# A Fourier and gated convolution kernel: where 64-bit weights are narrowed, and in how many operations

## The chip, the cores and the metric

The kernel runs on one core of a Trainium2 chip. The metric is device time in microseconds (us), as the median of several executions on the chip; a single profiled execution has a span, which is some 1.8 us shorter than its time. In the text TensorE, VectorE, ScalarE and GpSimd are the four compute engines; in the profile they are PE (and PEld for its weight loads), DVE, ACT and POOL. SP is the engine that issues most of the transfers.

## The reference, cut to what matters

```python
def _attn_ref(x):                        # x: 8 batches, 3136 positions, 256 features, float32
    X = np.fft.fft(x, axis=1)
    X = np.fft.fft(X, axis=2)
    return X.real.astype(np.float32)

def _moe_ref(x, w_in, conv_w, w_out):    # 256 -> 1024 -> 256, kernel of 3 along the positions
    h = np.maximum(x @ w_in, 0.0)
    conv_out = ...                       # three taps of h along the positions, per feature
    gate = 1.0 / (1.0 + np.exp(-conv_out))
    return (h * gate @ w_out).astype(np.float32)
```

The three weights arrive as 64-bit floats. The kernel works in 32-bit floats and has to narrow them itself: 256 x 1024 first weights, 3 x 1024 taps, 1024 x 256 second weights.

## The kernel before

The kernel first **folds** x of a batch by its symmetries (VectorE), multiplies the folded x with tables of cosines and sines (the DFT along the positions, TensorE, in nine units), and leaves a pair of matrices, pt and qt. The feature DFT is folded into the first weights: `G` is the product of a small DFT matrix `dm` with `win`. Then 256 **steps** follow: 8 batches x 4 chunks of positions x 8 groups of 128 hidden features. A step multiplies pt and qt with G (`pa`, `pb`), combines them into h, computes the taps, the sigmoid and the gate, and multiplies with the second weights `wout`. Folds and DFT of the next batch are spread over the steps of the batch before it, as work on the side.

The start, and the narrowing before the change:

```python
    def narrow(dst, raw, ng):            # ten operations, scratch tiles f, g, h
        ts, tt, st = ng.tensor_scalar, ng.tensor_tensor, ng.scalar_tensor_tensor
        ...
        ts(out=fi, in0=hi, scalar1=20, scalar2=0x7FF, op0=lsr, op1=ALU.bitwise_and)
        ts(out=fi, in0=fi, scalar1=896, scalar2=1151, op0=ALU.max, op1=ALU.min)
        ts(out=fi, in0=fi, scalar1=23, scalar2=-0x40000000, op0=lsl, op1=ALU.bitwise_xor)
        ts(out=gi, in0=hi, scalar1=-0x80000000, scalar2=None, op0=ALU.bitwise_and)
        st(out=fi, in0=fi, scalar=0x7FFFFFFF, in1=gi, op0=ALU.bitwise_and, op1=ALU.bitwise_or)
        ts(out=gi, in0=lo, scalar1=1, scalar2=None, op0=lsr)
        st(out=g, in0=gi, scalar=2.0 ** -51, in1=f, op0=ALU.mult, op1=ALU.mult)
        ts(out=hi_, in0=hi, scalar1=3, scalar2=0x7FFFF8, op0=lsl, op1=ALU.bitwise_and)
        tt(out=fi, in0=fi, in1=hi_, op=ALU.bitwise_or)
        tt(out=dst, in0=f, in1=g, op=ALU.add)

    ...
    for t in range(2):                   # first weights, whole rows: 1 MB each, first in ScalarE's queue
        todo += load_weight(win[t], words(moe_w_in)[t * P:(t + 1) * P].unsqueeze(1), nc.vector, nc.scalar)
    for h in range(2):
        for f in load_ops(0, h, nc.sync, nc.scalar):     # x of batch 0
            f()
    todo += load_weight(cw24, ...)       # taps
    nc.scalar.dma_start(out=dm, in_=dft_dim[:, :, 0:2])
    for par in (1, 0):
        load_tables(par)                 # odd tables, then even ones
    for f in todo:                       # narrow all first weights, then the taps
        f()
    late_w = load_weight(wout, words(moe_w_out)..., nc.vector, nc.sync)   # three blocks, for later
    for par in (1, 0):
        mend_tables(par, half)           # ScalarE copies of the odd tables
    ...                                  # G, ge, cw: all of them here
    for f in fold_ops(0):
        f()
    for h in range(2):
        for f in load_ops(1, h, nc.sync, nc.sync):
            f()
    begin, us, row = units(0)
    begin()
    for i, u in enumerate(us):           # DFT of batch 0
        u.matmuls(0, 1)
        u.copy()
        if i == 4:
            row()
        u.fin()
        if i == 4:
            spread(0)
        for g in late_w[i::len(us)]:     # a block of second weights after units 0, 1 and 2
            g()
```

`row` and `spread` carry one row of qt through DRAM and spread it over the partitions (`er`, `ed`, `eb`); each step's `pa` is seeded with it.

Of the kernel before, what the change touches and what calls it, by code (L numbers as in the profile page):

```python
# [10 lines left out]
I32 = mybir.dt.int32  # L11
AF = mybir.ActivationFunctionType
# [22 lines left out]
def kernel(  # L35
# [70 lines left out]
    def load_ops(b, h, eng, eng2):  # L106

        def plain():
            t = xp.tile([P, 8, 2, D], F32, name="xh", tag="xh")
            xh[b, h] = t  # L110
            eng.dma_start(out=t[0:NP, 0:4], in_=bass.AP(
                tensor=x.tensor, offset=x.offset + (b * S + 1 + 2 * h) * D,
                ap=[[HQ * D, NP], [Q4 * D, 4], [1, 2 * D]]))
            if h == 1:
                for s in range(8):
                    r = s if s < 4 else (8 - s) % 4
                    eng2.dma_start(out=t[NP:KR, s],
                                   in_=x[b:b + 1, r * Q4:r * Q4 + 1].to_broadcast([1, 2, D]))
# [248 lines left out]
    def narrow(dst, raw, ng):  # L367

        k, n = dst.shape

        ts, tt, st = ng.tensor_scalar, ng.tensor_tensor, ng.scalar_tensor_tensor
        lsl, lsr = ALU.logical_shift_left, ALU.logical_shift_right
        f, g, h = [hp.tile([P, HW], F32, name="nt", tag="h")[0:k, 0:n] for _ in range(3)]
        fi, gi, hi_ = [t.bitcast(I32) for t in (f, g, h)]
        lo, hi = raw[:, :, 0], raw[:, :, 1]

        ts(out=fi, in0=hi, scalar1=20, scalar2=0x7FF, op0=lsr, op1=ALU.bitwise_and)
        ts(out=fi, in0=fi, scalar1=896, scalar2=1151, op0=ALU.max, op1=ALU.min)
        ts(out=fi, in0=fi, scalar1=23, scalar2=-0x40000000, op0=lsl, op1=ALU.bitwise_xor)
        ts(out=gi, in0=hi, scalar1=-0x80000000, scalar2=None, op0=ALU.bitwise_and)  # L380
        st(out=fi, in0=fi, scalar=0x7FFFFFFF, in1=gi, op0=ALU.bitwise_and, op1=ALU.bitwise_or)

        ts(out=gi, in0=lo, scalar1=1, scalar2=None, op0=lsr)
        st(out=g, in0=gi, scalar=2.0 ** -51, in1=f, op0=ALU.mult, op1=ALU.mult)
        ts(out=hi_, in0=hi, scalar1=3, scalar2=0x7FFFF8, op0=lsl, op1=ALU.bitwise_and)
        tt(out=fi, in0=fi, in1=hi_, op=ALU.bitwise_or)
        tt(out=dst, in0=f, in1=g, op=ALU.add)

    def load_weight(dst, src, ng, eng):

        k, nc_, n = dst.shape
        if src.dtype == F32:
            eng.dma_start(out=dst, in_=src)
            return []
        raw = wp.tile([P, nc_ * n, 2], I32, name="raw", tag="w")[0:k]
        eng.dma_start(out=raw.rearrange("p (c n) e -> p c (n e)", c=nc_), in_=src)
        to = dst.rearrange("p c n -> p (c n)")
        w = nc_ * n
        parts = -(-w // HW)
        cuts = [slice(w * i // parts, w * (i + 1) // parts) for i in range(parts)]  # L400
        return [(lambda c=c: narrow(to[:, c], raw[:, c], ng)) for c in cuts]

    def words(w):
        return w if w.dtype == F32 else w.bitcast(I32)

    ident = gp.tile([3 * NF, 3 * NF], F32, name="ident", tag="g")
    make_identity(nc, ident)
    dm = gp.tile([P, 2, 2, P], F32, name="dm", tag="g")
    cw24 = gp.tile([3 * NF, 1, P], F32, name="cw24", tag="g")
# [4 lines left out]
    wout = const.tile([P, NF, D], F32, name="wout")  # L414
    win = pqp.tile([P, 2, F // 2 + 256], F32, name="win", tag="pt"), pqp.tile([P, 2, F // 2 + 256], F32, name="win", tag="qt")
    win = [t.rearrange("p a f -> p (a f)")[:, 0:F].unsqueeze(1) for t in win]
    todo = []
    for t in range(2):
        todo += load_weight(win[t], words(moe_w_in)[t * P:(t + 1) * P].unsqueeze(1), nc.vector, nc.scalar)
    for h in range(2):  # L420
        for f in load_ops(0, h, nc.sync, nc.scalar):
            f()
    todo += load_weight(cw24, words(moe_conv_w).rearrange("k (m p) -> (k m) p", m=NF).unsqueeze(1),
                        nc.vector, nc.scalar)
# [3 lines left out]
    for f in todo:  # L428
        f()
    late_w = load_weight(wout, words(moe_w_out).rearrange("(c p) o -> p c o", p=P), nc.vector, nc.sync)  # L430

    for par in (1, 0):
        mend_tables(par, half)
    G = const.tile([P, 2, F], F32, name="G")
    for g in range(2):
        for c in range(0, F, 512):
            p = psa.tile([P, 512], F32, name="pa", tag="pa") if g else spare()
            for t in range(2):
                mm(p, dm[:, t, g, :], win[t][:, 0, c:c + 512], t == 0, t == 1)
            nc.scalar.copy(out=G[:, g, c:c + 512], in_=p)  # L440

    ge = const.tile([P, NF], F32, name="ge")
    p = spare()
    for m in range(NF):
        for t in range(2):
            mm(p[:, m:m + 1], win[t][:, 0, m * P:(m + 1) * P], dm[:, t, 1, P - 1:P], t == 0, t == 1)
    nc.scalar.copy(out=ge, in_=p[:, 0:NF])
    cw = const.tile([P, 3, NF], F32, name="cw")
    p = spare()
# [80 lines left out]
    for f in fold_ops(0):  # L530
        f()
# [147 lines left out]
```

## Time and profile before

| | before |
|---|---|
| time, median of the first 3 runs | 1336.36 us (1335.93 to 1339.71) |
| span of the profiled run | 1334.3 us |
| PE, DVE, ACT, POOL busy | 91%, 88%, 66%, 35% |
| first h | 90.4 us (its second half stands in the chain of waits at 90.88) |
| length of batches 0 to 6, first h to first h | 165.9, 160.0, 157.9, 154.8, 154.8, 154.3, 147.9 us |
| batch 7 | 132.5 us from its first h to its last (31 steps), 148.3 to the end of the span |

The page names no engine that is full, because it averages a start, in which nearly everything waits, with a body, in which TensorE and VectorE are both almost full. So one reads the start and the body apart. The table of windows does this. Its columns are the window, its length, busy us (and instructions) of PE, PEld, DVE, ACT and POOL, the granted clock, the share of the transfer engines that is busy, and GB/s.

```profile
80.00:90.00 10.00, 1.40 (x2) 0.83 (x3) 0.79 (x2) 1.38 (x3) 3.22 (x7) 0.69 0.27 81
90.00:100.00 10.00, 6.22 (x10) 2.65 (x9) 9.52 (x12) 6.53 (x10) 1.86 (x2) 0.50 0.00 0
100.00:110.00 10.00, 8.29 (x21) 5.17 (x21) 9.93 (x14) 5.81 (x10) 3.46 (x7) 0.61 0.00 2
```

### The profile page before, as it was taken

The page shows a single profiled execution, that of the slowest core. Times are in us where ns is not written, and L with a number is a line of the kernel's source. Part 1 is how long each engine was busy: PE and PEld are TensorE (multiplying, and loading weights), DVE is VectorE, ACT ScalarE, POOL GpSimd, SP SyncE. Part 2 cuts the span into 40 slices and gives each one's busy share as a digit, 9 for nine tenths or more (in the row PEclk, how much of TensorE's full clock was granted, in tenths as well). Part 3 has the DMA queues.
Part 4 walks back from the last instruction along what each step waited for, and adds up shares of the span by engine and source line. Part 5 has one row for each costly group of instructions (what it writes and reads, how often), then busy time and mean ns, then how long its engine had stood idle before and what let it go on. Part 6 is the DMA issues. An engine that isn't in the chain of part 4 may idle for free.

```text
span 1334.3 us, 15340 instructions
## 1 busy us (share of the span) xinstructions
PE 1214.4 (91%) x4914; PEld 892.2 (67%) x4914; DVE 1175.9 (88%) x1664; ACT 887.0 (66%) x1558; POOL 462.1 (35%) x507
## 2 busy tenths in 40 slices
PE   0748899989899999999999999999999999999998
PEld 0425677767676777777676777767677777776766
DVE  6969999998998999998999899999899888878885
ACT  0225666667666677776767777776777767777775
POOL 2415525242532435242523335242332223222222
PEclk9968999999999999999999999999999999999999
DMA  7601202021120102120102102120001000100001
GB/s 227 176 25 37 85 25 65 32 64 35 54 67 24 52 26 71 49 75 25 60 13 74 50 25 73 48 75 0 25 24 48 27 24 25 34 30 22 24 20 43
DMA packets 46840, 66.02 MB, mean 49 GB/s; under 512 B 5600, under 2 KB 35196, under 8 KB 46504
## 3 DMA queue, kind: packets, MB, share of 16 engines
q1 hardware_dynamic: 41012, 49.80, 11.8%
q0 software_dynamic: 5120, 12.85, 3.2%
q10 hardware_dynamic: 628, 2.40, 0.6%
q8 instruction: 38, 0.62, 0.2%
q14 instruction: 42, 0.34, 0.1%
HBM read 39.24 MB, written 25.74 MB: 49 GB/s over the span
## 4 chain that ended last, share of the span: by engine, by line
DVE 50%; PE 22%; ACT 12%; issue 12%; DMA 3%; POOL 1%; DVEq 0%; ACTq 0%; POOLq 0%; SPq 0%
DVE g L498 16%; DVE h L486 15%; PE po L89 11%; ACT g L492 6%; PE pd L89 4%; DVE g L509 4%; PE pa L89 4%; PE pb L89 4%; DVE xh L158 3%; ACT os L525 2%; DVE xh L147 2%; DVE w L174 2%; DMA out_dram<-os 1%; ACT nb L485 1%; ACT pa L466 1%
## 5 line engine op out<-in xcount | busy, mean ns | idle before, releaser
L89 PE MATMUL po<-wout,g 128*128 128x256 f32 (+2 forms) x3200 | 735.9, 380 | 0.7 <-POOL g L508 0.7
L89 PEld LDWEIGHTS po<-wout,g 128*128 128x128 f32 (+2 forms) x3200 | 602.9, 188 | 149.1 <-issue 19.0
L498 DVE SCALAR_TENSOR_TENSOR g<-h,cw,g 128x770 f32<-128x770 f32 (+2 forms) x512 | 537.1, 1049 | 82.0 <-ACT g L492 72.3
L508 POOL TENSOR_TENSOR g<-g,h 128x385 f32<-128x385 f32 (+1 forms) x256 | 295.0, 1152 | 776.9 <-ACT g L501 634.1
L485 ACT ACTIVATE nb<-pb 128x386 f32<-128x386 f32 (+4 forms) x512 | 227.6, 499 | 147.2 <-PE pb L89 145.8
L501 ACT ACTIVATE g<-g 128x770 f32<-128x770 f32 (+2 forms) x256 | 221.1, 864 | 149.1 <-DVE g L498 148.6
L486 DVE CUSTOM_DVE_ANT_0 h<-pa,nb 128x386 f32<-128x386 f32 (+4 forms) x512 | 265.7, 561 | 50.4 <-PE pa L89 31.9
L492 ACT ACTIVATE g<-h,cw 128x770 f32<-128x770 f32 (+2 forms) x256 | 243.6, 952 | 46.9 <-DVE h L486 30.3
L89 PE MATMUL pa<-pt,G 128*128 128x386 f32 (+2 forms) x512 | 223.7, 518 | 43.8 <-ACT pa L466 43.6
L89 PE MATMUL pb<-qt,G 127*128 127x386 f32 (+2 forms) x512 | 215.8, 502 | 1.6 <-ACT nb L485 1.5
L89 PEld LDWEIGHTS pa<-pt,G 128*128 128x128 f32 x512 | 91.0, 191 | 144.7 <-ACT pa L466 101.4
L509 DVE TENSOR_TENSOR g<-g,h 128x385 f32<-128x385 f32 (+2 forms) x256 | 155.0, 606 | 0.5 <-ACT g L501 0.5
L466 ACT ACTIVATE pa<-eb,ge 128x386 f32<-128x386 f32 (+2 forms) x256 | 146.9, 574 | 8.1 <-DMA eb<-ed 8.1
L89 PE MATMUL pd<-tab,w 99*128 99x196 f32 (+2 forms) x448 | 123.1, 381 | 17.7 <-ACT g L492 6.1
L89 PEld LDWEIGHTS pb<-qt,G 127*128 127x128 f32 x512 | 94.7, 192 | 27.6 <-issue 4.5
L89 PEld LDWEIGHTS pd<-tab,w 99*128 99x128 f32 (+1 forms) x448 | 80.0, 189 | 44.7 <-ACT g L492 24.2
L122 POOL DMA_INDIRECT xh<-in_x_dram,idx x64 | 85.3, 1333 | 16.4 <-issue 12.2
L525 ACT COPY os<-po 128x256 f32<-128x256 f32 (+2 forms) x200 | 58.4, 384 | 13.5 <-DMA out_dram<-os 8.8
L158 DVE TENSOR_TENSOR xh<-xh 98x1024 f32<-98x1024 f32 (+1 forms) x32 | 51.1, 1603 | 0.1
L147 DVE TENSOR_TENSOR xh<-xh 98x1020 f32<-98x1020 f32 (+1 forms) x32 | 46.6, 1466 | 0.0
L89 PE MATMUL po<-win,dm 128*128 128x512 f32 x8 | 5.7, 872 | 38.9 <-DMA dm<-dft_dim_dram 38.9
L174 DVE TENSOR_TENSOR w<-xh 98x508 f32<-98x508 f32 (+1 forms) x32 | 37.5, 1172 | 0.1
(84 smaller groups left out, 352.8 us busy)
## 6 DMA issues: line engine op xcount, KB each, us to landing
out_dram<-os SPq DMA_DIRECT2D x184, 128.0 KB
xh<-in_x_dram SPq DMA_DIRECT2D x16, 784.0 KB
eb<-ed SPq DMA_DIRECT2D x16, 193.0 KB
tab<-dft_seq_dram SPq DMA_DIRECT2D x4, 601.8 KB
raw<-in_moe_w_in_dram ACTq DMA_DIRECT2D x2, 1024.0 KB
raw<-in_moe_w_out_dram SPq DMA_DIRECT2D x1, 2048.0 KB
eb<-ed SPq DMA_DIRECT2D x8, 209.0 KB
eb<-ed SPq DMA_DIRECT2D x8, 192.5 KB
```

The source lines that it names most:

```text
L89: nc.tensor.matmul(o, l, r, start=start, stop=stop, skip_group_check=True)
L122: nc.gpsimd.indirect_dma_start(out=xh[b, h][0:NP, 4 + m].rearrange("p q d -> p (q d)"), out_offset=None, in_=bass.AP(tensor=x.tensor, offs ...
L158: vt(flat(to, to + 2), flat(0, 2), flat(2, 4), op=op)
L466: act(pa[s][:, 0:n], eb[b, c], AF.Copy, scale=ge[:, f:f + 1])
L485: act(nb[:, i, cols], p[:, cols], AF.Copy, scale=-1.0 if i else 1.0)
L486: nc.vector._custom_dve(TENSOR_ADD_SAT, out=to, in0=a[:, cols], in1=nb[:, i, cols], s0=BIG, s1=0.0)
L492: act(gs[s], hs[s][:, 0:n], AF.Copy, scale=cw[:, 0, s[2]:s[2] + 1])
L498: stt(out=g, in0=h[:, k:k + n], scalar=cw[:, k, f:f + 1], in1=g, op0=ALU.mult, op1=ALU.add)
L501: act(gs[s], gs[s], AF.Sigmoid)
L508: gt(g[:, m:n], g[:, m:n], h[:, m + 1:n + 1], op=ALU.mult)
L509: vt(g[:, 0:m], g[:, 0:m], h[:, 1:m + 1], op=ALU.mult)
L525: nc.scalar.copy(out=osb[0:m, j % 2], in_=pt[0:m, j % 2])
```

## The change

Its intent: to start the folds as early as x is there. Only half of the first weights' columns is loaded and narrowed before the folds; the other half follows inside the DFT of batch 0, and the second weights only inside steps 1 to 8, a block of 256 columns in each. The ten operations become eight, which work in place in the raw words and in the destination. The loads stand in another order. Batch 1 is loaded and folded four steps later, and the windows of folds and DFT of the later batches move up to five steps.

```diff
-    def load_ops(b, h, eng, eng2):
+    def load_ops(b, h, eng):           # single rows ahead of the large load, all on SP's queue
...
+    def narrow(dst, raw):
+        ts = nc.vector.tensor_scalar
+        lo, hi = raw[:, :, 0], raw[:, :, 1]
+        lof, hif, d = lo.bitcast(F32), hi.bitcast(F32), dst.bitcast(I32)
+        ts(out=d, in0=hi, scalar1=20, scalar2=0x7FF, op0=lsr, op1=ALU.bitwise_and)
+        ts(out=d, in0=d, scalar1=-896, scalar2=0, op0=ALU.add, op1=ALU.max)
+        ts(out=d, in0=d, scalar1=23, scalar2=None, op0=lsl)
+        stt(out=d, in0=hi, scalar=-0x80000000, in1=d, op0=ALU.bitwise_and, op1=ALU.bitwise_or)
+        stt(out=lof, in0=lo.bitcast(U32), scalar=2.0 ** -52, in1=dst, op0=ALU.mult, op1=ALU.mult)
+        ts(out=hi, in0=hi, scalar1=3, scalar2=0x7FFFF8, op0=lsl, op1=ALU.bitwise_and)
+        vt(hi, hi, d, op=ALU.bitwise_or)
+        vt(dst, hif, lof, op=ALU.add)
...
+    w_in = Weight(win, moe_w_in.rearrange("(t p) n -> p t n", p=P), wp, "w")
+    w_in.load((0, 2), (0, H), nc.scalar)           # H = F // 2: half of the columns, one load
     for h in range(2):
-        for f in load_ops(0, h, nc.sync, nc.scalar):
+        for f in load_ops(0, h, nc.sync):
             f()
     nc.scalar.dma_start(out=dm, in_=dft_dim[:, :, 0:2])
     for par in (1, 0):
         load_tables(par)
+    w_cv.load((0, 1), (0, P), nc.scalar)
+    w_in.load((0, 2), (H, F), nc.scalar)           # the other half, one load
...
+    for t in range(2):
+        w_in.narrow(t, (0, H))
     for f in fold_ops(0):
         f()
-    for h in range(2):
-        for f in load_ops(1, h, nc.sync, nc.sync):
-            f()
+    w_cv.narrow(0, (0, P))
+    blocks(0)                                      # first half of G
+    for par in (1, 0):
+        mend_tables(par, half)
...                                                # in the DFT of batch 0:
         if i == 4:
             spread(0)
-        for g in late_w[i::len(us)]:
-            g()
+            taps()
+            w_in.narrow(0, (H, F))
+        if i == 6:
+            w_in.narrow(1, (H, F))
+    blocks(1)                                      # second half of G
+    w_out = Weight([wout[:, c] for c in range(NF)], moe_w_out..., wp, "w")
+    for c in range(0, NF, 2):
+        w_out.load((c, c + 2), (0, D), nc.sync)
...
+    for c in range(NF):
+        at(1 + c, "dve", lambda c=c: w_out.narrow(c, (0, D)))
+    for h in range(2):
+        for j, fn in enumerate(load_ops(1, h, nc.sync)):
+            at(3 * h + (j + 1) // 2, "load", fn)
...
-    end = 0
+    end = 4
     for b in range(1, B):
-        stop = per * (b - 1) + max(12 - 4 * (b - 1), 2)
+        stop = per * (b - 1) + max(21 - 4 * b, 2)
         fold_at[b] = (end, stop - end)
         dft_at[b] = (stop, per * b - 3 - stop)
```

More of the change, by code (lines that the diff above doesn't have):

```diff
@@ L11 @@
 I32 = mybir.dt.int32
+U32 = mybir.dt.uint32
 AF = mybir.ActivationFunctionType
@@ L110, in plain @@
             xh[b, h] = t
+            if h == 1:
+                for s in range(8):
+                    r = s if s < 4 else (8 - s) % 4
+                    eng.dma_start(out=t[NP:KR, s],
+                                  in_=x[b:b + 1, r * Q4:r * Q4 + 1].to_broadcast([1, 2, D]))
             eng.dma_start(out=t[0:NP, 0:4], in_=bass.AP(
@@ L113, in plain @@
                 ap=[[HQ * D, NP], [Q4 * D, 4], [1, 2 * D]]))
-            if h == 1:
-                for s in range(8):
-                    r = s if s < 4 else (8 - s) % 4
-                    eng2.dma_start(out=t[NP:KR, s],
-                                   in_=x[b:b + 1, r * Q4:r * Q4 + 1].to_broadcast([1, 2, D]))
         def mirrored(m):
@@ L363 @@
     HN = max(c.k1 - c.k0 for c in chunks)
-    def narrow(dst, raw, ng):
-        k, n = dst.shape
-        ts, tt, st = ng.tensor_scalar, ng.tensor_tensor, ng.scalar_tensor_tensor
+    def narrow(dst, raw):
+        ts = nc.vector.tensor_scalar
         lsl, lsr = ALU.logical_shift_left, ALU.logical_shift_right
-        f, g, h = [hp.tile([P, HW], F32, name="nt", tag="h")[0:k, 0:n] for _ in range(3)]
-        fi, gi, hi_ = [t.bitcast(I32) for t in (f, g, h)]
         lo, hi = raw[:, :, 0], raw[:, :, 1]
-        ts(out=fi, in0=hi, scalar1=20, scalar2=0x7FF, op0=lsr, op1=ALU.bitwise_and)
-        ts(out=fi, in0=fi, scalar1=896, scalar2=1151, op0=ALU.max, op1=ALU.min)
-        ts(out=fi, in0=fi, scalar1=23, scalar2=-0x40000000, op0=lsl, op1=ALU.bitwise_xor)
-        ts(out=gi, in0=hi, scalar1=-0x80000000, scalar2=None, op0=ALU.bitwise_and)
-        st(out=fi, in0=fi, scalar=0x7FFFFFFF, in1=gi, op0=ALU.bitwise_and, op1=ALU.bitwise_or)
-        ts(out=gi, in0=lo, scalar1=1, scalar2=None, op0=lsr)
-        st(out=g, in0=gi, scalar=2.0 ** -51, in1=f, op0=ALU.mult, op1=ALU.mult)
-        ts(out=hi_, in0=hi, scalar1=3, scalar2=0x7FFFF8, op0=lsl, op1=ALU.bitwise_and)
-        tt(out=fi, in0=fi, in1=hi_, op=ALU.bitwise_or)
-        tt(out=dst, in0=f, in1=g, op=ALU.add)
@@ L389, in load_weight @@
-    def load_weight(dst, src, ng, eng):
-        k, nc_, n = dst.shape
-        if src.dtype == F32:
-            eng.dma_start(out=dst, in_=src)
-            return []
-        raw = wp.tile([P, nc_ * n, 2], I32, name="raw", tag="w")[0:k]
-        eng.dma_start(out=raw.rearrange("p (c n) e -> p c (n e)", c=nc_), in_=src)
-        to = dst.rearrange("p c n -> p (c n)")
-        w = nc_ * n
-        parts = -(-w // HW)
-        cuts = [slice(w * i // parts, w * (i + 1) // parts) for i in range(parts)]
-        return [(lambda c=c: narrow(to[:, c], raw[:, c], ng)) for c in cuts]
@@ L403, in words @@
-    def words(w):
-        return w if w.dtype == F32 else w.bitcast(I32)
+        lof, hif, d = lo.bitcast(F32), hi.bitcast(F32), dst.bitcast(I32)
[4 more added lines that the diff above has]
+        stt(out=lof, in0=lo.bitcast(U32), scalar=2.0 ** -52, in1=dst, op0=ALU.mult, op1=ALU.mult)
@@ new lines, in narrow, with __init__, load @@
+        ts(out=hi, in0=hi, scalar1=3, scalar2=0x7FFFF8, op0=lsl, op1=ALU.bitwise_and)
+        vt(hi, hi, d, op=ALU.bitwise_or)
+        vt(dst, hif, lof, op=ALU.add)
+    class Weight:
+        def __init__(self, dst, src, pool, tag):
+            self.dst, self.src = dst, src
+            k, c, n = dst[0].shape[0], len(dst), dst[0].shape[1]
+            self.raw = None
+            if src.dtype != F32:
+                self.raw = pool.tile([P, c, n, 2], I32, name="raw", tag=tag)[0:k]
+                self.src = src.bitcast(I32)
+        def load(self, cs, cols, eng):
+            c0, c1 = cs
+            i0, i1 = cols
+            if self.raw is None:
+                for c in range(c0, c1):
+                    eng.dma_start(out=self.dst[c][:, i0:i1], in_=self.src[:, c, i0:i1])
+            else:
+                eng.dma_start(out=self.raw[:, c0:c1, i0:i1].rearrange("p c n e -> p c (n e)"),
+                              in_=self.src[:, c0:c1, 2 * i0:2 * i1])
+        def narrow(self, c, cols):
+            i0, i1 = cols
+            if self.raw is not None:
+                narrow(self.dst[c][:, i0:i1], self.raw[:, c, i0:i1])
@@ L406 @@
+    H = F // 2
     ident = gp.tile([3 * NF, 3 * NF], F32, name="ident", tag="g")
@@ L408 @@
     dm = gp.tile([P, 2, 2, P], F32, name="dm", tag="g")
-    cw24 = gp.tile([3 * NF, 1, P], F32, name="cw24", tag="g")
+    cw24 = gp.tile([3 * NF, P], F32, name="cw24", tag="g")
     half = const.tile([P, 1], F32, name="half")
@@ L413 @@
     nc.gpsimd.tensor_scalar(out=half, in0=half, scalar1=0.5, scalar2=0.5, op0=ALU.mult, op1=ALU.add)
-    wout = const.tile([P, NF, D], F32, name="wout")
-    win = pqp.tile([P, 2, F // 2 + 256], F32, name="win", tag="pt"), pqp.tile([P, 2, F // 2 + 256], F32, name="win", tag="qt")
-    win = [t.rearrange("p a f -> p (a f)")[:, 0:F].unsqueeze(1) for t in win]
-    todo = []
-    for t in range(2):
-        todo += load_weight(win[t], words(moe_w_in)[t * P:(t + 1) * P].unsqueeze(1), nc.vector, nc.scalar)
+    win = [pqp.tile([P, NK], F32, name="win", tag=tag)[:, 0:F] for tag in ("pt", "qt")]
+    w_in = Weight(win, moe_w_in.rearrange("(t p) n -> p t n", p=P), wp, "w")
+    w_in.load((0, 2), (0, H), nc.scalar)
     for h in range(2):
-        for f in load_ops(0, h, nc.sync, nc.scalar):
+        for f in load_ops(0, h, nc.sync):
             f()
-    todo += load_weight(cw24, words(moe_conv_w).rearrange("k (m p) -> (k m) p", m=NF).unsqueeze(1),
-                        nc.vector, nc.scalar)
     nc.scalar.dma_start(out=dm, in_=dft_dim[:, :, 0:2])
@@ L427, with blocks, taps @@
         load_tables(par)
-    for f in todo:
-        f()
-    late_w = load_weight(wout, words(moe_w_out).rearrange("(c p) o -> p c o", p=P), nc.vector, nc.sync)
-    for par in (1, 0):
-        mend_tables(par, half)
-    G = const.tile([P, 2, F], F32, name="G")
-    for g in range(2):
-        for c in range(0, F, 512):
+    w_cv = Weight([cw24], moe_conv_w.rearrange("k (m p) -> (k m) p", m=NF).unsqueeze(1), gp, "g")
+    w_cv.load((0, 1), (0, P), nc.scalar)
+    w_in.load((0, 2), (H, F), nc.scalar)
+    wout = const.tile([P, NF, D], F32, name="wout")
+    G = const.tile([P, 2, F], F32, name="G")
+    ge = const.tile([P, NF], F32, name="ge")
+    cw = const.tile([P, 3, NF], F32, name="cw")
+    def blocks(i):
+        c = slice(i * H, (i + 1) * H)
+        for g in range(2):
             p = psa.tile([P, 512], F32, name="pa", tag="pa") if g else spare()
             for t in range(2):
-                mm(p, dm[:, t, g, :], win[t][:, 0, c:c + 512], t == 0, t == 1)
-            nc.scalar.copy(out=G[:, g, c:c + 512], in_=p)
-    ge = const.tile([P, NF], F32, name="ge")
-    p = spare()
-    for m in range(NF):
-        for t in range(2):
-            mm(p[:, m:m + 1], win[t][:, 0, m * P:(m + 1) * P], dm[:, t, 1, P - 1:P], t == 0, t == 1)
-    nc.scalar.copy(out=ge, in_=p[:, 0:NF])
-    cw = const.tile([P, 3, NF], F32, name="cw")
-    p = spare()
-    mm(p[:, 0:3 * NF], cw24[:, 0], ident, True, True)
-    nc.scalar.copy(out=cw.rearrange("p k m -> p (k m)"), in_=p[:, 0:3 * NF])
+                mm(p, dm[:, t, g, :], win[t][:, c], t == 0, t == 1)
+            nc.scalar.copy(out=G[:, g, c], in_=p)
+        p = spare()
+        ms = slice(i * NF // 2, (i + 1) * NF // 2)
+        for m in range(ms.start, ms.stop):
+            for t in range(2):
+                mm(p[:, m:m + 1], win[t][:, m * P:(m + 1) * P], dm[:, t, 1, P - 1:P], t == 0, t == 1)
+        nc.scalar.copy(out=ge[:, ms], in_=p[:, ms])
+    def taps():
+        p = spare()
+        mm(p[:, 0:3 * NF], cw24, ident, True, True)
+        nc.scalar.copy(out=cw.rearrange("p k m -> p (k m)"), in_=p[:, 0:3 * NF])
     rows = out.rearrange("b s d -> (b s) d")
@@ L527, in mm2 @@
         gs.pop(s)
+    for t in range(2):
+        w_in.narrow(t, (0, H))
     for f in fold_ops(0):
         f()
-    for h in range(2):
-        for f in load_ops(1, h, nc.sync, nc.sync):
-            f()
+    w_cv.narrow(0, (0, P))
+    blocks(0)
+    for par in (1, 0):
+        mend_tables(par, half)
     begin, us, row = units(0)
@@ L544 @@
             spread(0)
-        for g in late_w[i::len(us)]:
-            g()
+            taps()
[3 more added lines that the diff above has]
+    blocks(1)
+    w_out = Weight([wout[:, c] for c in range(NF)], moe_w_out.rearrange("(c p) o -> p c o", p=P), wp, "w")
+    for c in range(0, NF, 2):
+        w_out.load((c, c + 2), (0, D), nc.sync)
     steps = [(b, c, f) for b in range(B) for c in range(len(chunks)) for f in range(NF)]
@@ L569 @@
                 c1 = cs[7 * h + 6] + 1
-                for j, fn in enumerate(load_ops(b + 1, h, nc.sync, nc.sync)):
+                for j, fn in enumerate(load_ops(b + 1, h, nc.sync)):
                     at(c1 + (j + 1) // 2, "load", fn)
```

## The prediction

> **What bounds the kernel now.** I read the page's strip of 40 slices first. In it a digit is the busy share of 33 us.
>
> ```profile
> PE   0748899989899999999999999999999999999998
> DVE  6969999998998999998999899999899888878885
> ```
>
> From the fourth slice on both TensorE (PE) and VectorE (DVE) are nearly full, so the body is a balance; the loose time is in slices one to three. So next the timeline of the start (start us, duration us, engine, line, operation, tiles, idle before it).
>
> ```profile
> 7.95 0.61 DVE L377 TENSOR_SCALAR nt<-raw 128x512 int32<-128x512 int32 x1 [7.95 <-DMA raw<-in_moe_w_in_dram]
> 8.59 0.43 DVE L378 TENSOR_SCALAR nt<-nt 128x512 int32<-128x512 int32 x1
> ...
> 12.83 0.69 DVE L387 TENSOR_TENSOR win<-nt 128x512 f32<-128x512 f32 x1
> 13.44 0.42 DVE L377 TENSOR_SCALAR nt<-raw 128x512 int32<-128x512 int32 x1
> ...
> 34.53 2.33 DVE L147 TENSOR_TENSOR xh<-xh 98x1020 f32<-98x1020 f32 x2
> ...
> 40.28 3.36 ACT L211 ACTIVATE tab<-tab 99x784 f32<-99x784 f32 x4 [8.60 <-DMA tab<-dft_seq_dram]
> ...
> 51.98 8.70 PE L89 MATMUL po<-tab,w 99*128 99x196 f32 x32 [0.17 <-POOL w L178]
> ...
> 60.59 0.87 DVE L387 TENSOR_TENSOR wout<-nt 128x682 f32<-128x682 f32 x1
> 61.37 0.56 DVE L289 TENSOR_TENSOR qt<-as,po 128x392 f32<-128x392 f32 x1
> ```
>
> DVE narrows the 64-bit first weights from 8 to 29.4, waits for the taps, and only at 34.5 starts the folds of batch 0, which end at 51.8 (17.3 us). DFT matmuls start at 52 and are then paced by DVE, which slips three blocks of second weights, 7.25 us each, between their results. From the chain of waits, what follows (start, duration, who):
>
> ```profile
> 77.13 1.91 DMA er<-qt
> 79.17 0.53 POOL er L317
> ...
> 84.53 3.41 DMA eb<-ed
> 87.97 0.59 ACT pa L466
> 88.60 1.67 PE pa L89 x2
> 90.88 0.55 DVE h L486
> ```
>
> The first of 256 steps computes h at 90.88. The path to it is DVE, then a row that travels through DRAM. Now the body, again in the chain of waits:
>
> ```profile
> 105.53 1.02 DVE h L486 x2
> ...
> 110.79 1.01 DVE h L486 x2
> ...
> 1213.03 1.03 DVE h L486 x2
> ...
> 1217.11 1.03 DVE h L486 x2
> ```
>
> A step with one fold operation takes 5.26 us, a bare one 4.08. The table of windows has DVE busy 9.93 of 10 us in 100-110, 120-130 and 130-140 alike: in the first steps DVE is the bound, without slack. By first h of each batch, batches last 165.9, 160.0, 157.9, 154.8, 154.8, 154.3, 147.9 and some 132.5 us: with neither folds nor DFT 132.5; the DFT adds about 15.4, and folds add some 7 when they run beside a DFT but 14.4 (12 x 1.2) in batch 0, where they run alone.
>
> [...] reads of raw (every second word) take 0.42 us, no more than contiguous ones, and the stores into qt, also every second word, take 0.56 us for 392 elements, what 1.07 ns per element plus 0.15 gives. [...] The large table loads have 49 rows[...]: the windows show 176 GB/s and DMA share 0.44 (7/16) at 22-27, where they run alone. [...] here the granted clock was 0.82 to 0.84 in 50-80 and 0.50 in 90-100, so I take DFT durations from this start and not from the body.
>
> **The change part by part.**
> 1. *Eight operations for ten.* Four one-source and four two-source operations: at 512 columns 4 x 0.43 + 4 x 0.69 = 4.48 us in place of 5.30. At 256 columns, from 0.21/0.28 us at 128 columns and 0.43/0.69 at 512, I estimate 0.28 and 0.42, so 2.80 us a block. All narrowing: 4 x 4.48 + about 2.0 (taps) + 8 x 2.80 = 42.3 us, against 4 x 5.30 + 2.4 + 3 x 7.25 = 45.4. Only 3 us are truly removed; the rest moves.
> 2. *Start.* The first half of the first weights is again 1 MB at the head of its queue, but its runs are half as long, beside x in another queue: 9.5 us (an estimate, from 8 before). Two blocks end at 18.5; by then the first half of x, requested first, should be there. Folds run straight on, 17.3 us, to 36. The other candidate is the tables: each of seven engines carries 2.4 MB/7 = 343 KB of them, plus its share of x, weights and dm, some 350 KB; at 176/7 = 25 GB/s this is 28 us after the first issue, plus waits of later loads for earlier ones: landed at 34. The four table copies (3.7) bring this to 38. Tables are the later: DFT starts at 38, not 52.
> 3. *DFT.* Units 0 to 3 take 8.7 us as before, now with no second weights between: qt complete at 48 (copy 0.33 and two adds 0.9), not 76.8. The row's way takes 11.2 us as before, to 59: no longer last. What is last is DVE: 4.48 of narrowing (52.5), two results (54.4), 4.48 again (58.8); then TensorE builds the second half of G: one 512-column product at 0.85, two more 1.7, and half of the one-column products, which took 3.6 us for all, 1.85: 4.4 us (63.2). The earlier products need only what is ready before. The copy, seed and first products take 2.2: **first h at 65.5, so 25 us earlier**.
> 4. *Second weights inside steps 1 to 8.* 8 x 2.80 = 22.4 us of DVE, where DVE is the bound: bare steps of some 6.8 and fold steps of some 8. I count **22 us back**.
> 5. *Folds of batch 1 four steps later, its DFT in 12 steps for 17*, and later folds start up to five steps later in their batch, so more of them run without a DFT beside them. Five steps at 0.6 us of fold, of which half was hidden, is 1.5 us each in batches 1 and 2, less later and partly returned in batch 0: **2 us back** with the denser DFT.
> Sum: 1336.4 - 25 + 22 + 2 = 1335.4. I round to 1335.
>
> **The rivals.**
> *A: the start's gain stays.* If TensorE were the true bound of the whole, narrowing in steps 1 to 8 would be hidden and 20 us or more kept: 1312 to 1316. For it: TensorE is 91% busy and DVE 88%. Against it: 9.93 of 10 us on DVE in just these steps, and a step there follows every added DVE operation.
> *B: tables or weights land late.* The second half of the first weights waits for x, and the last tables for that; landing at 42 in place of 34 makes 1343. For it: ScalarE already waited 8.6 us for tables, until 40.28. Against it: that queue had idle waits and here has fewer.
> *C: strided operations run slow.* [...] The stores into qt speak against it.
> *D: the first products wait for second weights.* They are loaded only after the first ones are read. I expect the first 512 KB at 68, needed by DVE at 71: hidden, but close.
>
> **Range and chances.** The uncertain terms are the first h (4 us either way), what the narrowing costs the steps (3) and the later batches (3); together some 6, and a wider range for what I don't see: 1323 to 1346. Two per cent is 26.7 us; A alone nearly reaches it, B and C together hardly do. Faster 0.03, same 0.95, slower 0.02.
>
> **What would show it.** In the profile after: folds start near 18.5 and end near 36; DFT matmuls start near 38 with ScalarE's table copies as the last to end before them; the first h near 65; narrowing operations of 256 columns at 0.28 and 0.42 us; steps 1 to 8 lasting 6.8 to 8 us with DVE full; first h of batch 1 near 255, where before it was 256.3, so the gain is gone by then; later batches within 2 us of theirs. I am wrong if steps 1 to 8 last hardly longer than 5.3 us, if first h is off by over 5 us, or if a wait for a load appears ahead of the folds or the first second-weight block.

Five passages are cut out and marked. What the estimates rest on was measured in the kernel before: at 512 elements VectorE's operations with one source take 0.43 us and those with two 0.69; the 1.07 ns per element and the 0.15 us are an estimate from two sources at 128 elements (0.28 us) and at 512 (0.69 us). The seven engines of the tables are an estimate from the window 22 to 27, in which the 16 transfer engines were busy 0.44 of the time, as much as seven of them, at 176 GB/s.

## The result, and the profile after

The changed kernel takes 1359.39 us (median of 4 runs, 1357.48 to 1359.77), the kernel before 1336.14 us (4 runs, 1333.98 to 1339.71). The ratio is 1.0168, with a 95% interval of 1.0144 to 1.0193: clearly slower, by less than 2%, and 13 us outside the range that I had given. A ratio here is the mean time of one kernel's runs over that of the other's in the same rounds, so it isn't quite the ratio of the medians.

By first h of each batch, the span of 1355.7 us is made up like this:

| | before | after | difference |
|---|---|---|---|
| first h of batch 0 | 90.4 | 75.1 | -15.3 |
| batch 0 | 165.9 | 191.1 | +25.2 |
| batch 1 | 160.0 | 161.6 | +1.6 |
| batch 2 | 157.9 | 159.9 | +2.0 |
| batch 3 | 154.8 | 162.0 | +7.2 |
| batches 4 to 7 and the end | | | +0.7 |
| span | 1334.3 | 1355.7 | +21.4 |

I had expected -25, +22 and, for all the rest, +2. So the start gained too little, and batch 3 lost something that I hadn't seen at all.

**The start.** The timeline of the changed kernel (start us, duration us, engine, line, operation, tiles, and in brackets the idle time before it and what ended it):

```profile
9.96 0.43 DVE L376 TENSOR_SCALAR win<-raw 128x512 int32<-128x512 int32 x1 [9.96 <-DMA raw<-in_moe_w_in_dram]
...
13.86 0.69 DVE L384 TENSOR_TENSOR win<-raw 128x512 f32<-128x512 f32 x1
...
21.35 0.43 DVE L376 TENSOR_SCALAR win<-raw 128x512 int32<-128x512 int32 x1 [6.80 <-DMA raw<-in_moe_w_in_dram]
...
25.86 2.34 DVE L148 TENSOR_TENSOR xh<-xh 98x1020 f32<-98x1020 f32 x2
...
38.37 3.31 ACT L212 ACTIVATE tab<-tab 99x784 f32<-99x784 f32 x4 [4.60 <-DMA tab<-dft_seq_dram]
...
43.32 8.97 PE L90 MATMUL po<-tab,w 99*128 99x196 f32 x32 [10.71 <-POOL w L179]
...
65.96 2.07 PE L90 MATMUL po<-win,dm 128*128 128x512 f32 x2 [4.03 <-DVE win L384]
...
67.83 3.55 PE L90 MATMUL pa<-win,dm 128*128 128x512 f32 x4
...
71.22 1.84 PE L90 MATMUL po<-dm,win 128*128 128x1 f32 x16
...
75.09 1.02 DVE L493 CUSTOM_DVE_ANT_0 h<-pa,nb 128x385 f32<-128x385 f32 x2 [7.71 <-PE pa L90]
```

The first block is narrowed in 4.6 us, as worked out. The second block, whose bytes came with the same load, waits 6.8 us, until 21.35, for a transfer of first weights. In the recorded trace the semaphore on which this operation waits is the one that the load issued at 12.20 raises, the load of the *other* half of the columns (the load of its own half, issued at 0.74, has another, which released the first block at 9.96). The other half's load writes rows t=0 and t=1 at once, so, seen as one stretch from its first to its last byte in a partition, it covers the first half of t=1. The kernel's dependence tracking appears to see it as that one stretch; the operation reads none of its bytes. The folds therefore start at 25.9 in place of 18.5, and the DFT at 43.3 in place of 38. The tables are late too: their copies start at 38.4, not 34. At the end, the second half of G takes from 65.96 to 73.06, 7.1 us for the 4.4 worked out. TensorE had idled 4.03 us before it, and the granted clock in just this stretch was 0.63 (4.4/0.63 is 7.0).

**Steps 1 to 8.** Step 3 of the changed kernel, with the part of GpSimd that runs at the same time:

```profile
94.01 1.15 POOL L515 TENSOR_TENSOR g<-g,h 128x385 f32<-128x385 f32 x1 [5.80 <-ACT g L508]
...
94.36 0.95 DVE L376 TENSOR_SCALAR wout<-raw 128x256 int32<-128x256 int32 x1
95.35 0.33 DVE L377 TENSOR_SCALAR wout<-wout 128x256 int32<-128x256 int32 x1
...
97.62 0.43 DVE L384 TENSOR_TENSOR wout<-raw 128x256 f32<-128x256 f32 x1
...
97.96 2.07 DVE L505 SCALAR_TENSOR_TENSOR g<-h,cw,g 128x769 f32<-128x769 f32 x2
...
99.95 1.02 DVE L493 CUSTOM_DVE_ANT_0 h<-pa,nb 128x385 f32<-128x385 f32 x2
```

A block takes 3.6 us from its start to the start of the next group (94.36 to 97.96), for the 2.80 estimated. Seven of its operations are close to the estimated durations (0.29 to 0.33, and 0.43). The first takes 0.95 for 0.28: it ends at 95.31, just after GpSimd's half of the gate ends at 95.16. It is the same at 101.35 and 110.68: the first operation takes 0.95 and 0.99 us and ends 0.15 to 0.2 us after the gate. What holds it until then the trace doesn't show; below I call it a wait. But this wait isn't all new: in a bare step VectorE idles 0.6 us at this place anyway, for ScalarE's first tap, and in a fold step the fold operation had the wait (in the kernel before, one of 1024 elements took 1.89 us at 101.74, where GpSimd's gate ran from 101.38 to 102.54; at the start, without a gate, two of this size took 2.36 together). Steps 1 to 8 last 6.51, 6.99, 6.99, 9.33, 8.13, 8.09, 8.21 and 8.18 us, that is, but for step 4, 2.4 to 3.0 us more than a bare step (4.08) or a step with a fold (5.25). The lengths went as predicted. Step 4 holds two fold operations beside its block (2.34 and 0.17 us); VectorE was busy 9.11 of its 9.35 us, so that TensorE worked at a clock of 0.63 there is not what held it.

**Batch 3.** Steps 115 to 117 last 6.1, 5.0 and 8.3 us; their neighbours last 4.1 to 5.7. What stands there, from the timeline:

```profile
678.07 1.02 POOL L318 TENSOR_TENSOR er<-as 1x197 f32<-1x197 f32 x1 [6.60 <-DMA er<-qt]
...
690.56 0.97 POOL L123 DMA_INDIRECT xh<-in_x_dram,idx  x1 [0.31 <-issue]
691.28 2.39 DVE L516 TENSOR_TENSOR g<-g,h 128x385 f32<-128x385 f32 x1
...
691.56 1.69 POOL L515 TENSOR_TENSOR g<-g,h 128x385 f32<-128x385 f32 x2
...
694.36 1.56 PE L90 MATMUL pd<-tab,w 98*128 98x392 f32 x4 [2.96 <-DVE as L280]
...
698.24 3.25 PE L90 MATMUL po<-wout,g 128*128 128x256 f32 x12
```

GpSimd idles 6.6 us, until 678.07, for the row of qt: its small transfer was issued at 673.09, right behind the 784 KB load of batch 6 (672.68). Then GpSimd computes the feature row of batch 4, to 682.9, and after it issues four gathers of x for batch 6 between its gates. Its gate is late; VectorE's own gate operation takes 2.39 us for 0.55; TensorE then waits 2.96 us for a DFT result, and works the next products more slowly: pb took 1.41 us there for 0.82 nine us earlier, pa 1.49 for 0.92, and the twelve products with wout 3.25 for 2.75, at a granted clock of 0.83 from 694.4 to 704.3 (1.00 from 680 to 690). In the kernel before, gathers and feature row of the same batches meet as well: two gathers at 653.25 and 655.17, the row from 656.17 to 661.3, two more gathers at 662.23 and 663.66. But GpSimd has no such idle time there, and steps 112 to 115 last only 4.5, 5.6, 4.7 and 4.1 us. So it isn't enough that the two meet; the order in which they come, and the late row, differ.

### The profile page after: what moved, and what is told of

It is laid out like the page before. It is cut to its first block, busy times and chain, and to the rows that moved or that the text cites. A ratio compares the mean times of both kernels' runs of the same rounds, so it can differ in the third digit from the quotient of the medians.

```text
span 1355.7 us, 15365 instructions
## 1 busy us (share of the span) xinstructions
PE 1226.4 (90%) x4914; PEld 894.8 (66%) x4914; DVE 1177.4 (87%) x1688; ACT 885.8 (65%) x1559; POOL 460.9 (34%) x507
## 4 chain that ended last, share of the span: by engine, by line
DVE 47%; PE 25%; issue 13%; ACT 12%; DMA 2%; POOL 1%; ACTq 0%; DVEq 0%; POOLq 0%; SPq 0%
DVE h L493 15%; DVE g L505 14%; PE po L90 12%; ACT g L499 6%; PE pd L90 5%; PE pa L90 4%; DVE g L516 4%; PE pb L90 4%; ACT os L532 3%; DVE xh L159 2%; DVE xh L148 2%; DVE w L175 2%; ACT nb L492 1%; DMA out_dram<-os 1%; ACT pa L473 1%
## 5 line engine op out<-in xcount | busy, mean ns | idle before, releaser
L505 DVE SCALAR_TENSOR_TENSOR g<-h,cw,g 128x770 f32<-128x770 f32 (+2 forms) x512 | 534.9, 1045 | 85.0 <-ACT g L499 75.4
L90 PE MATMUL pa<-pt,G 128*128 128x386 f32 (+2 forms) x512 | 226.9, 525 | 60.8 <-ACT pa L473 60.3
L177 POOL COPY w<-xh 98x4 f32<-98x4 f32 (+1 forms) x32 | 26.9, 840 | 31.1 <-DVE xh L164 31.1
```

What stands on the lines that cost most here:

```text
L90: nc.tensor.matmul(o, l, r, start=start, stop=stop, skip_group_check=True)
L505: stt(out=g, in0=h[:, k:k + n], scalar=cw[:, k, f:f + 1], in1=g, op0=ALU.mult, op1=ALU.add)
```

## The experiments

Each kernel ran on a chip beside the kernel before, in three rounds (the last one in five). All gave correct results.

### Only the later windows as before

```diff
-        stop = per * (b - 1) + max(21 - 4 * b, 2)
+        stop = 17 if b == 1 else per * (b - 1) + max(16 - 4 * b, 2)
```

> The changed kernel, but the folds and DFTs of batches 2 to 7 stand in the same steps as before the change (batch 1 keeps its later fold window). In the changed kernel batches 1, 2 and 3 lasted 161.6, 159.9 and 162.0 us, against 160.0, 157.9 and 154.8 before. Theory that the shifted windows cost this: the three go back to about 160, 158 and 155, so about 10 us are regained and the run takes 1349. Rival, that those batches are slow because of what the start leaves behind (clock, late loads): nothing changes, 1359.

Measured: 1346.95 us (before, on the same chip as the other three of this group: 1338.02), ratio to before 1.0078 [1.005, 1.0106]. First h at 75.3; batches 190.9, 161.2, 157.6, 154.7. Batches 2 and 3 are what they were before the change, batch 1 hardly moved. Its 1.2 us above the kernel before lie in steps 32 to 35, where the folds of batch 2, whose window is still the squeezed one, stand in other steps; from step 36 on it is as before, step by step. The moved windows cost some 10 us of the changed kernel's 21, and this holds by batch, not only in the sum.

### Batch 3: five loads four steps later

```diff
-                c1 = cs[7 * h + 6] + 1
+                c1 = cs[7 * h + 6] + (5 if b == 5 and h == 0 else 1)
```

> The changed kernel, but the first five loads of batch 6 come four steps later, so that the gathers that GpSimd issues do not fall on the steps in which GpSimd computes the feature row of batch 4. In the changed kernel three steps there (115 to 117 of the 256) lasted 6.1, 5.0 and 8.3 us. Theory that this collision makes batch 3 last 162.0 us for 154.8: batch 3 goes back to 155 to 157, the run takes 1353. Rival, that the denser DFT of batch 4 (24 steps for 27) does it: batch 3 stays near 162, 1359.

Measured: 1354.45 us, ratio 1.013 [1.0105, 1.0155]. Batch 3 lasts 156.8 us in place of 162.0; steps 115 to 117 last 5.2, 4.1 and 5.3. Nothing was removed, five loads were only moved by four steps. So 5.2 of the 7.2 us come from where these loads stand. But they are one large load and four gathers, and the edit changes two things. The gathers leave the steps of the feature row; and the row's transfer no longer stands behind the large load in SP's queue, where that load waited for its place. It is issued at 662.19 in place of 673.09, and GpSimd starts the row 4.9 us earlier:

```profile
673.17 0.91 POOL L318 TENSOR_TENSOR er<-as 1x197 f32<-1x197 f32 x1 [1.58 <-ACT as L310]
```

The run doesn't separate the two, and moving the gathers alone was not tried. The other 2 us are not the denser DFT either: in this trace, as in that of the changed kernel, steps 97 and 99 are 1.2 us longer each than in the kernel before. Fold operations of batch 4 stand there, which the shift has moved into batch 3, and the DFT begins only in step 101; from step 100 on the batch is 0.3 us shorter than before.

### The second half of the first weights in two loads

```diff
-    w_in.load((0, 2), (H, F), nc.scalar)
+    for t in range(2):
+        w_in.load((t, t + 1), (H, F), nc.scalar)
```

> The changed kernel, but the second half of the first weights comes in two loads, one for each 128 rows, so that the second narrowing block no longer waits for bytes that it does not read. In the changed kernel this wait was 6.8 us (14.55 to 21.35) and folds began at 25.9. Theory: folds begin near 19 and end near 36.5; but the copies of the tables waited until 38.4 for the last table and end at 41.7, so the DFT starts at about 42 in place of 43.3, and the first h is only 1 to 2 us earlier (73 to 74): 1357. Rival, that the wait costs its full length: first h near 68, 1352.

Measured: 1356.43 us, ratio 1.0147 [1.012, 1.0175]; first h at 72.5, 2.6 us earlier. The second block now follows the first without a gap (14.36), folds run from 18.9 to 36.1, as the prediction had it. But they don't set the DFT. The copies of the tables do, in this kernel's timeline:

```profile
37.30 3.24 ACT L212 ACTIVATE tab<-tab 99x784 f32<-99x784 f32 x4 [6.03 <-DMA tab<-dft_seq_dram]
...
40.59 8.94 PE L90 MATMUL po<-tab,w 99*128 99x196 f32 x30 [3.26 <-ACT tab L212]
```

The wait of 6.8 us was real and worth only 2.6, because a second one stood right behind it.

### Odd and even tables in two tiles as well

```diff
-    tab = const.tile([P, 6, HQ, HE], F32, name="tab")
+    tabs = (const.tile([P, 2, HQ, HE], F32, name="tabe"), const.tile([P, 4, HQ, HE], F32, name="tabo"))
...                                       # every use of tab[:, s] takes the tile of its parity
```

> As split_load (first h at 72.5), and the tables are two tiles, odd and even, so that the copies of the odd ones no longer wait for the even ones, which land last. In split_load folds ended at 36.1, the last copy at 40.5, and the DFT began at 40.6. Theory that the tables held it there: the copies start at about 31.7 and end at 35, DFT starts at about 36.5, first h at about 68.5, 1352. Rival, that DFT start isn't what sets the first h (the even tables then hold the third unit, or VectorE's narrowing does): first h stays at 71 to 72.5, 1356.

Measured: 1352.45 us, ratio 1.01 [1.0075, 1.0125]; first h at 68.3. From its timeline:

```profile
30.87 3.32 ACT L213 ACTIVATE tabo<-tabo 99x784 f32<-99x784 f32 x4
...
36.41 6.23 PE L90 MATMUL po<-tabo,w 99*128 99x196 f32 x16 [10.64 <-DVE cw L377]
```

The copies read and write odd tables alone. With one tile for all they had waited for the last even one, although none of its bytes concerns them; with two tiles they run 6.4 us earlier, and then the folds set the DFT. Both needless waits together cost the changed kernel 6.8 us of first h, where it came 9.6 us later than predicted.

### Only the eight operations, in the kernel before

```diff
-        ...                              # the ten operations
+        ...                              # the eight in-place operations, same blocks, same places
```

> The kernel before, with only the eight in-place operations in place of the ten, in the same places and block sizes. Each 512-column block 4.48 us for 5.30, each 682-column block 5.56 for 7.25, taps 2.0 for 2.4: 8.8 us of VectorE less, nearly all on the path to the first h. Theory that this part gains by itself and what loses is the moving and cutting up: first h near 83, 1328. Rival, that stores to every second word run slow: each block at 5.3 us or more, 1336. Second rival, that the loads hold the start: first weights done earlier but folds no earlier than 33, then 1331.

Measured: 1333.89 us, ratio 0.9976 [0.9952, 1.0], so the time alone hardly tells it from the kernel before; first h at 87.2, 3.2 us earlier than in the profile of before; all batches as before. The operations have the durations worked out (0.43 and 0.69 us at 512 columns, 0.51 and 0.87 at 682), the same as contiguous ones at 512 columns in the kernel before (0.43 and 0.69), so the stores to every second word cost nothing that shows here. VectorE is busy 36.0 us with narrowing for 42.2 before, 6.2 less and not the 8.8 expected: the expectation took 7.25 us for an old block of 682 columns, and the traces of the kernel before show 6.7. But of the first weights' gain nothing arrives:

```profile
25.52 0.69 DVE L383 TENSOR_TENSOR win<-raw 128x512 f32<-128x512 f32 x1
...
32.29 0.21 DVE L375 TENSOR_SCALAR cw<-raw 24x128 int32<-24x128 int32 x1 [6.08 <-DMA raw<-in_moe_conv_w_dram]
```

VectorE is done 3.2 us earlier than before (25.5 + 0.7, where it was 29.4) and waits 3.4 us longer for the taps (6.08 for 2.70), which stand late in their queue. The gain that remains comes from the second weights. It is the second rival of the expectation that held in mechanism; its 1331 was a little too good.

### Second weights in four wide blocks

```diff
-    for c in range(NF):
-        at(1 + c, "dve", lambda c=c: w_out.narrow(c, (0, D)))
+    for c in range(0, NF, 2):
+        at(1 + c, "dve", lambda c=c: narrow(<columns of c and c + 1 as one block of 512>))
```

> The changed kernel, but the second weights are narrowed in four blocks of 512 columns, in steps 1, 3, 5 and 7, in place of eight of 256 in steps 1 to 8. In the changed kernel a 256-column block took 3.47 us: seven operations as I worked out (2.5 us) and the first one 0.92 to 0.99 for 0.28, which ends when GpSimd's part of the gate ends. Theory that fixed cost per operation and this wait once a block make the second weights dear: a block takes 4.48 + 0.65 = 5.1 us, four 20.5 in place of 27.8, batch 0 lasts 184 and the run 1351. Rival, that the steps are held by something else (TensorE at half clock, the loads of batch 1): batch 0 stays near 190, 1358.

Measured: 1353.45 us, ratio 1.0118 [1.0093, 1.0143]; batch 0 lasts 184.6 us, 6.5 less, with first h where it was (74.9). Half of the work's operations vanish and none of its elements: the same bytes in 32 operations instead of 64. So cutting the second weights into eight blocks costs 6.5 us by itself. Blocks of 512 columns took 4.6 to 5.3 us. The half clock of the rival was there: in the changed kernel the granted clock was 0.50 from 75 to 88. But in step 3 (92.96 to 99.95) it was 1.00, and that step lasted its 6.99 us all the same.

### Second weights before the first step

```diff
+    w_out = Weight([wout[:, c] for c in range(NF)], moe_w_out..., xp, "xh")   # in the place of x
...
+    late = {0: pair(0), 1: pair(2), 7: pair(4), 8: pair(6)}   # blocks of 512 after these DFT units
...
+    for f in load_ops(1, 1, nc.sync):    # second half of x of batch 1, before the first step
+        f()
...                                       # windows of batches 1 to 7 as before the change
```

> The changed kernel, but the second weights are narrowed before the first step, in four blocks of 512 columns between the results of the first DFT, their words held where x of batch 1 comes later; batch 1 is loaded and folded in the same steps as before the change, and so are all later windows. Theory that VectorE has some 12 us of idle time between folds and first h that can take part of this work, while in steps 1 to 8 it has none: first h comes at 79 to 82 (75.1 in the changed kernel), but batch 0 goes back to 166 and batches 1 to 3 to 160, 158, 155: 1326. Rival, that the start is bound by the second half of G and the row, and all 18 us are added there: first h at 90, 1336.

Measured: 1331.51 us, ratio 0.9948 [0.9921, 0.9975]; first h at 81.3; batches 169.5, 160.0, 157.9, 154.8. In the steps the narrowing made the steps up to step 16 longer by 19.4 us than before the change, and by 13.8 us in the same blocks of 512 (wide_blocks); the rest of batch 0's 25 us lies in steps 17 to 31, with the denser DFT. In the start it costs 6.2 us of first h (and 3.7 us in step 0, of which more below), since VectorE had idle time there: it was busy 7.17 us of the 15 from 60 to 75 in the changed kernel, and 15.35 of the 16 from 60 to 76 here. The second half of G takes 4.4 us (71.0 to 75.4). The granted clock was 0.93 from 60 to 76 here and 0.63 in the stretch of 7.1 us in the changed kernel, so I put the difference down to the clock. I had expected 1326; the difference is mostly step 0, which lasts 8.95 us:

```profile
86.83 0.19 POOL L489 MEMSET h<- 128x2 f32 x3
86.98 0.94 ACT L499 ACTIVATE g<-h,cw 128x769 f32<-128x769 f32 x1 [9.78 <-POOL h L489]
...
87.95 2.08 DVE L505 SCALAR_TENSOR_TENSOR g<-h,cw,g 128x769 f32<-128x769 f32 x2 [3.31 <-ACT g L499]
```

GpSimd writes the zeros at the edges of h only after four gathers that wait for the raw words' place, and everything else waits for the zeros.

### Both together

> early_wout and split_both together. Theory: both gains add, first h 4 to 6 us earlier than in early_wout, at 74 to 77, later batches as before the change: 1321. Rival, that with the second weights in the start VectorE alone is the bound there and an earlier DFT only makes TensorE wait: first h within 2 us of early_wout, 1325.

The edit joins the two before. Measured: 1328.75 us, ratio 0.9936 [0.9908, 0.9964]; first h at 79.0, only 2.2 us earlier than early_wout, close to what the rival said. But its reason isn't what the trace shows. The DFT starts 6.9 us earlier than in early_wout (36.46), and then VectorE idles 5.4 us for its first result:

```profile
43.71 0.36 DVE L279 TENSOR_TENSOR as<-as,po 128x196 f32<-128x196 f32 x1 [5.43 <-ACT as L275]
```

ScalarE copies this result only after it has corrected the even tables, and these now arrive later (it corrects them at 42.4, in split_both at 36.8). That the second weights, loaded beside them, make them late is argued, not shown.

### The gathers of batch 1 in steps 0 to 2

```diff
-    for f in load_ops(1, 1, nc.sync):
-        f()
+    for j, fn in enumerate(load_ops(1, 1, nc.sync)):
+        at((j + 1) // 2, "load", fn)
```

> early_split, but the last five loads of batch 1 (second half of x) are issued in steps 0 to 2 in place of before the first step. In early_wout and early_split step 0 lasted 8.95 us, against 5.27 before the change: VectorE waited for ScalarE's first tap, which needs the zeros that GpSimd writes at the edges of h, and GpSimd had four gathers ahead of them. Theory that this is the wait: step 0 goes back to about 5.3, first h stays near 79, 1325. Rival, that step 0 is long because the clock is at half or because TensorE's second seed is late: it stays near 9, 1329.

Measured: 1326.15 us, ratio 0.9933 [0.9905, 0.9962]; step 0 lasts 5.26 us and batch 0 165.9. First h is at 77.8.

### The start in another order

```diff
+        if i < 2:
+            w_in.narrow(i, (H, F))       # second halves during the first two DFT units
         u.fin()
+        if i == 1:
+            mend_tables(0, half)         # even tables corrected after the second unit
         if i == 4:
             spread(0)
             taps()
-            w_in.narrow(0, (H, F))
-        if i == 6:
-            w_in.narrow(1, (H, F))
-    blocks(1)
+            blocks(1)                    # second half of G after the feature row
+        if i in late:                    # late = {4: pair(0), 5: pair(2), 7: pair(4), 8: pair(6)}
+            late[i]()
```

> best_fix with the start put in another order: the second halves of the first weights are narrowed right after the folds, while TensorE works on the first two DFT units (VectorE idled 5.4 us there in early_split); the second half of G is built after the feature row in place of at the end; and the correction of the even tables stands after the second unit, so that ScalarE's first copy does not wait for them. Theory that VectorE then idles hardly at all between folds and first h: from 36.2, taps 2, halves 9, results 8, second weights 18 make 73 to 75 for the first h, 1320. Rival, that the row or the even tables now hold it: first h at 78 to 79, 1325.

Measured in five rounds: 1321.98 us (1318.16 to 1322.66), before 1336.96, ratio 0.9879 [0.9857, 0.9901]. First h at 74.6, right at the end of the last block of second weights:

```profile
73.99 0.69 DVE L385 TENSOR_TENSOR wout<-raw 128x512 f32<-128x512 f32 x1
74.60 1.02 DVE L495 CUSTOM_DVE_ANT_0 h<-pa,nb 128x385 f32<-128x385 f32 x2
```

First h comes as early as in the changed kernel (75.1), but here all weights are narrowed by then, and the batches last what they lasted before the change (batch 2 alone 159.8 for 157.9). It beats both kernels: the change's early folds and its eight operations were worth having, and its place for the second weights was not.

## Why the prediction was wrong

The mechanism that the prediction is built on held: the start gains, and steps 1 to 8 give it back. But they give back more than there was: the first h of batch 1 comes at 266.2, where 255 was predicted and 256.3 was measured before the change. Two of the prediction's own signs of being wrong came true: the first h is off by over 5 us, and a wait for a load stands ahead of the folds. Two terms of the sum were mis-sized most. By the table of batches, in which the sum is off by 22 us, they make 18.5; the second weights add 3.2.

- **Step 2 and 3, the start: -25 predicted, -15.3 measured.** The step that failed is "Folds run straight on, 17.3 us, to 36", and with it "landed at 34" for the tables. Folds did take 17.2 us, but started 7.4 us late, behind a wait on bytes that the operation doesn't read; the DFT began 5.3 us late. The tables' copies would have held it to about 41 even so (split_load), for they waited for tables that they don't use. The other terms of the 9.6 us: narrowing operations that took up to 1.1 us while GpSimd worked on the feature row, 1.8 us from DFT start to their end; second half of G at low clock (0.63), 2.7 us; and 0.2 us less after that. Removing both waits brought 6.8 us (split_both), more than 5.3, since the DFT then starts at 36.4 and not at the predicted 38. Rival B had named late loads, with 34 moved to 42, so its kind was foreseen; I held it for unlikely because I looked at how fast bytes arrive and not at which load each operation waits for. The order of the built program, which names these semaphores, was there to be read.
- **Step 5, the later batches: +2 predicted, some +11 measured** (1.6 + 2.0 + 7.2). I had priced folds that no DFT hides and not looked at what else moves into the same steps. old_windows regains the 2.0 and the 7.2; loads_apart shows that in batch 3 5.2 us come from where five loads stand, and its trace that the remaining 2 are unhidden folds, which the prediction had priced too low. Whether the gathers or the row behind the large load make the 5.2 us stays open. For batch 2 the shift costs some 2 to 4 us: it lasted 159.9 to 161.7 us in the five kernels that have the moved windows, and 156.4 to 157.9 in six of the seven that have those of before (the seventh, the best kernel, is at 159.8, and why isn't known).
- **Step 4, second weights in the steps: +22 predicted, +25.2 measured for batch 0**, which also holds the denser DFT of batch 1. Steps 0 to 16 alone are 19.4 us longer than before the change, and steps 17 to 31, where that DFT runs, 5.8. The expected 6.8 and 8 us a step were measured as 6.5 to 7.0 and 8.1 to 8.2. Right in mechanism, but that the size fits is partly luck: a block takes 3.6 to 3.7 us and not 2.80, and some 0.8 us of it cost nothing (6.99 - 4.08 is 2.9), the wait of 0.6 us that a bare step has anyway among them.
- **Step 1, eight operations for ten: right for each operation, wrong in the sum.** 0.43/0.69 us at 512 columns and 0.29/0.43 at 256; rival C, slow strided operations, is refuted. But "only 3 us are truly removed" (45.4 to 42.3) has the wrong sign: VectorE was busy 42.2 us with narrowing before the change and 49.0 after it. The old blocks of second weights took 6.7 us and not 7.25, and the eight new ones 3.7 and not 2.80. In the old blocks eight operations save 6.2 us of VectorE and 3.2 us of first h (eight_ops_only); that the second weights are cut into eight blocks takes 6.5 us back (wide_blocks).
- The 132.5 us that the prediction gives for a batch with neither folds nor DFT are 31 steps and not 32. With another bare step it is 136.6, so the DFT adds some 11 us and not 15.4. The sum doesn't use this.
- **Rival A** (TensorE is the true bound, and narrowing in the steps is hidden) is refuted by the lengths of steps 1 to 8. **Rival D** didn't come about: the second weights were there when they were needed.

The two errors pointed the same way, so a range that treated them as independent was too narrow. The range also had no room for something that isn't in the sum at all, such as batch 3.

## What to carry to other kernels

Before moving work, ask of both places whether the engine that does it idles there: here 18 us of narrowing cost 6 us of first h in the start, and 14 us in steps in which VectorE was full (9.93 of 10 us busy before the change; 19 us in smaller blocks). When a start is rearranged, read for each operation which load's semaphore it waits for; a load that fills two separate stretches, or a tile that holds two sets of tables, can make an operation wait for bytes that it never reads (both together cost 6.8 us of first h here), and a second wait may stand right behind the first. A schedule by step numbers that is shifted "a little" can change the order in which side work meets in a queue or on an engine; look at each batch's length, not only at the sum.
